# Zero products in TensorE's gaps, a K/V contraction in 256 columns, and a new order: grouped attention and a gated MLP with their gradients, on one core

## The chip, the cores and the metric

One NeuronCore of one Trainium2 chip. The time is device microseconds of one execution, median of several; lower is better. The core has TensorE (PE, with weight loads listed apart as PEld), VectorE (DVE), ScalarE (ACT), GpSimd (POOL) and SyncE (SP), which here issues nearly all DMAs from one queue. TensorE writes to PSUM; ScalarE and VectorE copy from there to SBUF ("eviction"), and DMAs move data between SBUF and the chip's main memory.

## What is computed

The forward pass of a decode block and its gradients for a given `grad_out`:

```
xn = layernorm(x)                                  # x: 2 x 1 x 576
q  = xn @ wq                                       # 32 query heads of 128, 16 K/V heads
o  = softmax(q k^T / sqrt(128)) v                  # K, V: 2 x 16 x 4096 x 128
out = x + o @ wo + ((xn @ w_gate) * (xn @ w_up)) @ w_down
outputs: out, d x, d k_cache, d v_cache, d wq, d wo, d w_gate, d w_up, d w_down
```

With one query token per batch entry there is little arithmetic for each byte. K and V (32 MB each) are read once, their gradients (32 MB each) are written once, and so are the weights and their gradients: 92.48 MB are read and 92.48 MB written.

## The kernel before

**Work.** There are 16 steps `s`, each for one batch entry and a group of two K/V heads. A step loads two K tiles and two V tiles of 1 MB (`load_kv`), turns them with VectorE's 32x32 transposes (`turn`, line 1156), forms scores with K and dP with V on TensorE (`score`, line 1205, 32 products of 128 columns for one head), does the softmax and its gradient in small instructions of all engines (`softmax`, `dscore`), and then two kinds of larger work:

- `contract(s, t)` (lines 1361 to 1400): P times V for the output (t = 1) and dS times K for dq (t = 0). Sixteen products of 512 columns run in two parts of eight (line 1378), four side by side in column groups of 32. They write the PSUM tile `ct`; an eviction of 512 columns takes it to `osb`, and four small products with the constant `fold` (line 1395) sum it up. After the products the K or V tiles are free for the next load (`free_kv`).
- `outer` and `head_outer` (line 1226): the gradients of K and V, outer products of 512 columns into a PSUM tile of two banks, evicted in 1024 columns (lines 422 and 424) to a 1 MB tile that SP stores (`put`, line 644).

The projections and the MLP (`group_front`, `group_back`, `mlp`) have the same form: weights are loaded, products are formed, the weights' gradients are outer products (lines 675, 712, 756 and others) and are stored. PSUM has three tiles `o` of two banks and two tiles `m` of one bank; all 1 MB tiles of loads and stores come from one ring of 16 (`big`).

**Order.** Nothing is ordered by hand. Every piece of work is a generator that yields what it needs: an engine with a cost in microseconds (`PE`, `ACT`, `DVE`, `POOL`, `EV` for an eviction on the engine that is done earlier), a DMA, a ring's slot (`ACQ`, `REL`), an event (`WAIT`, `SET`). `Order.run` (line 153) replays them in a model of time when the kernel is built: of the streams that can go on it takes the earliest, and among those of one engine within a slack the one with the best priority (`PRI`, lines 256 to 293; `AT` says after which K/V load a weight's load goes). The instructions are emitted in that order, and on the chip each engine and SP's queue keep it. Real waits are by semaphores, which follow from the tiles that an instruction reads and writes; the replay's times only set the order. A product's cost in the replay is

```
def PE(stream, issue=0.0, quad=None, kind="f"):
    return ("op", "PE", max(CLK * stream, issue) + 0.03, quad, stream, issue, kind)
```

where `stream` is the time at TensorE's full clock and `CLK` is 1.65 (line 301). `EV(512)` is billed at 0.585 us on ScalarE (line 222).

Of the kernel before, what the change touches and what calls it, by code (L numbers as in the profile page):

```python
# [13 lines left out]
P = 128  # L14
# [13 lines left out]
class Stream:  # L28
    def __init__(self, gen, prio, ready):
        self.gen, self.prio, self.ready = gen, prio, ready  # L30
        self.req = None
        self.land = None

# [30 lines left out]
class Order:  # L64
# [3 lines left out]
    def __init__(self):  # L68
# [8 lines left out]
        self.lanes = []  # L77

# [74 lines left out]
    def run(self):  # L153
        while self.streams:
# [12 lines left out]
            if r[0] in ("op", "any"):  # L167
                cost = r[2] if r[0] == "op" else next(c for x, c, _ in r[1] if x == e)
                quad = r[3] if len(r) > 3 else None
                if e == "PE":  # L170
                    end = t + cost + self.TAIL
# [7 lines left out]
                s.ready = end + self.HOP  # L179
# [4 lines left out]
            elif r[0] == "acq":  # L184
# [3 lines left out]
                i = min((k for k, v in slots.items() if v is not None), key=lambda k: (when(slots[k]), k))  # L188
                slots[i] = None
# [59 lines left out]
def DMA(engine, cost, nbytes, row=8192):  # L249
# [7 lines left out]
    "turn0": [12127.5, 6592.3, 21769.7, -2605.1, 16027.7, 11327.0, 15999.3, 39550.4, 10382.6, -7734.4, 35538.2,  # L257
        24878.1, 2718.9, 31584.2, -26890.5, 2784.8],
    "turn1": [-17638.3, 2610.3, 11642.0, -23025.1, -666.2, 15183.7, -8429.9, 1153.7, -20487.3, 25941.4,
        10117.7, 4947.3, -2272.2, 26485.5, 30929.5, -2450.0],  # L260
    "W0": [17499.7, 23187.9, 23229.4, -24562.1, -25413.4, 21241.8, -52583.1, 25355.3, -4026.7, -26992.9,
        -2792.0, -39509.0, -20712.1, -23397.7, -38581.5, -1973.1],
    "W1": [-68220.0, -3785.6, -5692.6, -26672.7, -32830.2, -16110.0, -12761.0, -19860.2, 22087.6, 15126.8,
        -21980.3, 8805.5, -32643.6, 50340.4, -9766.7, -46949.6],
    "BD0": [33847.1, 15885.5, -3782.4, -11229.3, 24201.3, 31507.4, 16705.2, 36715.7, 22613.4, -26234.1,
        -2581.7, 109848.8, -44765.9, -8040.0, -3442.2, 23039.7],
    "BD1": [6023.1, 63457.9, 25871.9, 3200.3, 32198.5, -18814.1, 12365.4, 26532.9, 45847.1, -51895.6, 27362.3,
        -76393.3, 2863.2, -15443.1, -42340.1, -14044.7],
    "att": [-30329.0, -12134.6, -9680.1, 2262.2, -4349.2, 5413.2, -20317.8, -14023.7, -15815.4, -22206.1,
        -49797.4, -334.9, -19593.2, -20211.8, -68161.8, -27358.0],  # L270
    "dsc": [-23906.4, -34630.7, -2728.5, -23998.0, -19328.5, -8575.3, -10061.5, -15550.8, 13655.4, -23902.2,
        -28324.1, -40880.7, -28538.6, -56867.0, -5830.5, -12006.5],
    "conv": [-12341.8, -11809.0, -28772.8, 4652.6, -75297.7, -7012.1, -20664.5, 17461.5, 27449.8, 21658.4,
        -6850.8, -13921.3, -10206.6, -13431.8, 19855.6, -8570.5],
    "con": [-42900.2, 17788.3, 198.2, -17106.1, -21976.4, -3999.9, 7207.3, -22623.4, -6927.6, 21516.2, 20924.0,
        -13390.2, -118243.2, -7700.5, 19019.7, 14780.5],
    "out0": [22678.2, 12788.2, 42398.2, 31027.3, 49279.4, -11087.6, 5917.5, 42793.0, -20399.7, 57105.8,
        29375.6, 687.4, 24906.2, -2550.4, -27276.1, 33869.5],
    "out1": [19262.8, 2604.4, 2928.7, 23228.2, 21627.8, -10501.4, 15188.8, 7961.4, 18967.4, 20607.5, 11898.0,
        33332.1, 33685.2, 22220.0, 30731.2, 4846.1],  # L280
    "load": [27975.6, -31596.9, -27237.7, 3512.0, -22563.4, -17007.1, 4137.9, 25122.5, 5758.3, -9052.6,
        -35105.2, 2003.7, -28928.7, 6812.9, 23298.4, -60102.7],
# [6 lines left out]
    "wout": [-3917.3],  # L289
    "store": [6257.1],  # L290
    "fin": [-45349.8],
    "const": [46567.9],
}
AT = {
    "wq": [-5, 7, 11, 24, 31, -18, 50, -5],
# [5 lines left out]
CLK = 1.65  # L301
# [1232 lines left out]
```

## Time and profile before

| | |
|---|---|
| median of 3 runs | 472.44 us (471.49 to 472.63) |
| the profiled execution | 471.37 us |
| its span, first to last instruction | 469.6 us |
| mean granted TensorE clock | 0.71 |
| bytes moved by DMA | 185.96 MB, mean 396 GB/s |
| products on TensorE | 6636, each with a weight load |

Busy times are of the span. "PEclk" is the clock that TensorE was granted; in this trace it is 0.5 or 1.0 at any moment. "DMA" is the mean busy share of the core's 16 DMA engines; packets that overlap can bring it a little over 1. A "wait" is idle time of an engine put down to what ended it; "SPq" is SP's queue, whose waits are those of the DMAs to be issued. Matmuls are pipelined, so a product's time holds its way through the array, and bursts are better compared whole.

### The profile page before, as it was taken

What the parts mean: (1) busy time and instruction counts of PE and PEld (TensorE: products, weight loads), DVE (VectorE), ACT (ScalarE), POOL (GpSimd) and SP (SyncE); (2) the same over time, 40 slices, a digit from 0 to 9 for tenths busy, and PEclk for the clock granted to TensorE, in tenths of its full rate; (3) what the DMA queues carried; (4) which work ended last, traced back from release to release, by engine and by line L of the source; (5) the groups of instructions that cost most, each with busy time, mean ns of one, the idle gap of its engine ahead of it and who ended that gap; (6) DMA issues with size and microseconds to landing.
All of it is one profiled execution on the core that took longest, in us unless ns stands there. A gap on an engine that the chain in (4) does not pass through costs nothing.

```text
span 469.6 us, 15459 instructions
## 1 busy us (share of the span) xinstructions
PE 370.8 (79%) x6636; PEld 217.5 (46%) x6636; DVE 369.5 (79%) x705; ACT 334.3 (71%) x507; POOL 146.8 (31%) x176
## 2 busy tenths in 40 slices
PE   0588688869887777986997669789699898998984
PEld 0455444435653352554463444564345434444453
DVE  9689878967867879688689658978867978898772
ACT  2149668867885948671798638877678678789973
POOL 3350242681330320203252264000843705325100
PEclk9978897767757668776675767956656658566977
DMA  8999999999999999999999999999999989999995
GB/s 317 404 413 403 363 390 419 409 416 421 418 416 420 399 421 406 412 415 419 399 418 404 386 418 424 408 413 342 413 416 393 424 270 416 423 413 413 424 368 176
DMA packets 40053, 185.96 MB, mean 396 GB/s; under 512 B 3496, under 2 KB 11184, under 8 KB 23600
## 3 DMA queue, kind: packets, MB, share of 16 engines
q1 hardware_dynamic: 39976, 184.96, 98.1%
q8 instruction: 52, 0.85, 0.7%
q14 instruction: 17, 0.14, 0.1%
q10 hardware_dynamic: 8, 0.00, 0.0%
HBM read 92.48 MB, written 92.48 MB: 394 GB/s over the span
## 4 chain that ended last, share of the span: by engine, by line
PE 42%; ACT 18%; DVE 18%; DMA 12%; issue 5%; POOL 2%; SPq 2%; ACTq 0%; DVEq 0%; POOLq 0%
ACT big L422 15%; DMA out_dram<-big 10%; DVE big L418 8%; PE ps_m L1378 8%; PE ps_o L1226 7%; PE ps_m L1205 7%; PE ps_o L675 4%; PE ps_m L841 3%; DVE big L424 3%; DMA big<-in_A_v_cache_dram 3%; PE ps_m L967 2%; PE ps_m L636 2%; POOL BD L1193 2%; PE ps_o L712 1%; SPq L1129 1%
## 5 line engine op out<-in xcount | busy, mean ns | idle before, releaser
L422 ACT CAST big<-ps_o 128x1024 bf16<-128x1024 f32 (+4 forms) x319 | 279.7, 950 | 40.3 <-PE ps_o L1226 18.2
L418 DVE STREAM_TRANSPOSE big<-big 128x1024 f32<-128x1024 f32 x146 | 176.1, 1223 | 5.9 <-DMA big<-in_A_v_cache_dram 3.6
L1193 POOL TENSOR_TENSOR BD<-vr,mask 128x2048 bf16<-128x2048 bf16 x32 | 115.2, 3603 | 198.8 <-ACT vr L422 122.2
L424 DVE CAST big<-ps_o 128x1024 bf16<-128x1024 f32 (+2 forms) x71 | 78.2, 1102 | 15.8 <-PE ps_o L675 5.2
L1205 PE MATMUL ps_m<-big,W 128*32 128x128 bf16 x2048 | 57.1, 274 | 5.5 <-ACT osb L422 0.7
L1226 PE MATMUL ps_o<-BD,dd 32*128 32x512 bf16 x256 | 48.8, 489 | 12.7 <-ACT big L422 9.2
L1205 PEld LDWEIGHTS <-W 128*32 128x32 bf16 x2048 | 45.4, 121 | 21.9 <-issue 18.6
L1226 PE MATMUL ps_o<-BD,pp 32*128 32x512 bf16 x256 | 42.1, 461 | 10.4 <-ACT big L422 6.7
L1170 POOL COPY W<-rep 32x16 bf16<-32x16 bf16 x128 | 24.5, 192 | 63.5 <-DVE rep L951 53.2
L418 DVE STREAM_TRANSPOSE big<-ww 128x1152 f32<-128x1152 f32 (+1 forms) x25 | 32.9, 1317 | 4.5 <-DMA out_dram<-big 3.3
L1378 PE MATMUL ps_m<-big,pp 128*32 128x512 bf16 x256 | 28.2, 536 | 1.5 <-DVE small L1330 1.2
L1378 PE MATMUL ps_m<-big,dd 128*32 128x512 bf16 x256 | 27.5, 518 | 1.5 <-DVE dd L418 0.6
L1226 PEld LDWEIGHTS <-dd 32*128 32x128 bf16 x256 | 11.8, 97 | 32.4 <-issue 24.7
L1226 PEld LDWEIGHTS <-pp 32*128 32x128 bf16 x256 | 10.4, 95 | 26.9 <-issue 22.6
L422 ACT CAST osb<-ps_m 128x512 bf16<-128x512 f32 x15 | 8.9, 590 | 15.9 <-PE ps_m L1378 12.6
L675 PE MATMUL ps_o<-dyr,R 32*32 32x288 bf16 x256 | 17.3, 402 | 2.0 <-ACT big L422 2.0
L675 PE MATMUL ps_o<-dyr,hb 32*32 32x288 bf16 x288 | 16.5, 346 | 1.1 <-ACT big L422 0.9
L967 PE MATMUL ps_m<-big,Wdy 128*128 128x128 bf16 x144 | 14.9, 285 | 3.1 <-DVE small L1283 2.0
L712 PEld LDWEIGHTS <-xnr 32*128 32x128 bf16 x368 | 12.5, 119 | 9.3 <-issue 8.6
L422 ACT CAST sp<-ps_m 128x256 bf16<-128x256 f32 x22 | 8.4, 380 | 11.2 <-PE ps_m L1213 11.0
L636 PEld LDWEIGHTS <-wm 128*32 128x32 bf16 x704 | 13.4, 115 | 6.3 <-issue 5.1
L841 PE MATMUL ps_m<-big,Wdy 128*128 128x128 bf16 x162 | 15.6, 272 | 0.6 <-DVE small L1291 0.4
(210 smaller groups left out, 481.9 us busy)
## 6 DMA issues: line engine op xcount, KB each, us to landing
out_dram<-big SPq DMA_DIRECT2D x74, 1024.0 KB, 12.1
big<-in_A_k_cache_dram SPq DMA_DIRECT2D x32, 1024.0 KB, 12.4
big<-in_A_v_cache_dram SPq DMA_DIRECT2D x32, 1024.0 KB, 12.5
out_dram<-big SPq DMA_DIRECT2D x17, 576.0 KB, 11.4
ww<-in_B_w_down_dram SPq DMA_DIRECT2D x9, 576.0 KB, 11.1
ww<-in_A_wo_dram SPq DMA_DIRECT2D x8, 576.0 KB, 11.1
ww<-in_A_wq_dram SPq DMA_DIRECT2D x8, 512.0 KB, 11.6
big<-in_B_w_gate_dram SPq DMA_DIRECT2D x4, 1024.0 KB, 13.1
```

What stands on the lines that cost most here:

```text
L418: nc.vector.transpose(out, in_)
L422: nc.scalar.copy(out, in_)
L424: nc.vector.tensor_copy(out=out, in_=in_)
L636: nc.tensor.matmul(dp[32 * q:32 * q + 32, :], lhsT=view(Wm[:], 0, P, 8 * pos(q, s), [[1, 32]]), rhs=view(X, 0, P, xoff(q, s), [[FS, blocks ...
L675: nc.tensor.matmul(o[32 * q:32 * q + 32, aa, 0:HD2], lhsT=view(t, 32 * q, 32, 2 * A + aa, [[4, 32]]), rhs=dyr[32 * q:32 * q + 32, k * HD2: ...
L841: nc.tensor.matmul(dh, lhsT=Wdy[:, e, 2 * k:2 * k + P], rhs=view(X[:], 0, P, 64 * k + e, [[D, FC], [2, 32]]), start=(k == 0 and e == 0), s ...
L967: nc.tensor.matmul(dp, lhsT=Wdy[:, e, 2 * k:2 * k + P], rhs=view(X[:], 0, P, 64 * k + e, [[D, GH], [2, 32]]), start=(k == 0 and e == 0), s ...
L1170: nc.gpsimd.tensor_copy(view(W_t[t][w][:], 32 * a, 32, 6 + 8 * a, [[G * WW, 4], [WW, G], [1, 2]]), view(rep_t[grp[g]["qs"]][:], 32 * a, 32 ...
L1193: nc.gpsimd.tensor_tensor(BD_t[i][:], view(vr_t[v][:], 0, P, 0, [[0, 16], [1, Dh]]), view(mask16[:], 0, P, 0, [[1, 16], [0, Dh]]), ALU.mult)
L1205: nc.tensor.matmul(sc[32 * cq:32 * cq + 32, :], lhsT=view(W[:], 0, P, (be * G + l) * WW + 6 - 4 * c2 - 2 * l, [[1, 32]]), rhs=view(X[:], 0 ...
L1226: nc.tensor.matmul(o[:, k, :], lhsT=pr2[32 * c4:32 * c4 + 32, :], rhs=BD[32 * c4:32 * c4 + 32, 8 * l + 4 * h2:8 * l + 4 * h2 + 4, :], star ...
L1378: nc.tensor.matmul(ct[32 * j:32 * j + 32, :], lhsT=view(rT, 0, P, 4 * c + 2 * l, [[1, 32]]), rhs=kv_t[kvS[s][t][l]][:, Dh * c:Dh * (c + 4) ...
```

## The change

Three things are changed together.

*Zero products.* Ahead of each group of products, `Order.run` looks for an idle gap of TensorE in the replay and for a PSUM tile (`m` or `o`) that is free in it, or the tile that the stream has just taken. It emits `keep`: products of a stationary of zeros (`none`, 128x128) with four copies of the identity, 512 columns, into that tile. Their number is 0.8 of the gap, less 0.05 us, over 0.1079 x CLK us, at most 40. The replay's times do not change by it.

*The contraction.* It runs in 256 columns in place of 512: 32 products in place of 16, `osb` half as wide, an eviction of 256 columns, and two products with `fold`. In the replay it also waits for the landing of its K or V tiles (`kvL`).

*The order.* All priorities, three of the slacks and biases, and the places of the weights' loads have new values. A column of PSUM that the softmax uses moves from 256 to 128.

```diff
@@ class Order
+        self.idle, self.spare, self.fill = 0, None, lambda tag, i, n: None
...
                 if e == "PE":
+                    self.idle = 0
+                    spare = [(self.slots[g][i], g, i) for g in ("m", "o") for i in self.slots[g] if self.slots[g][i] is not None]
+                    spare = min(spare + s.own, key=lambda x: x[0], default=None)
+                    if spare:
+                        gap = t - max(self.free[e], spare[0]) - FILL[0]
+                        self.idle = min(40, int(FILL[1] * gap / (FILL[2] * CLK))) if gap > 0 else 0
+                        self.fill(spare[1], spare[2], self.idle)
+                        self.spare = spare[1:] if spare not in s.own else None
                     end = t + cost + self.TAIL
...
-                s.ready = end + self.HOP
+                s.ready, s.own = end + self.HOP, []
...
+                s.own = [(slots[i], r[1], i)] if r[1] in ("m", "o") else []
                 slots[i] = None
...
 PRI = {
-    "turn0": [12127.5, 6592.3, 21769.7, ...
+    "turn0": [9201.5, 2578.1, 27143.9, ...
...
 AT = {
-    "wq": [-5, 7, 11, 24, 31, -18, 50, -5],
-    "wo": [-13, -2, -15, 2, 36, -14, 47, 53],
-    "mlp": [2, 16, -13, 39, 111],
+    "wq": [-8, 6, 9, -14, 30, 18, 42, 29],
+    "wo": [0, 3, -18, -19, -3, 14, 49, -5],
+    "mlp": [2, 17, 29, 40, 125],
 }
...
-BIAS = 0.21111771427708687
-SLACK = {"PE": 0.0, "ACT": 0.11786185086953341, "DVE": 0.44815392421950667, "POOL": 1e9, "SP": 1e9}
+FILL = (0.05, 0.8, 0.1079)
+BIAS = 0.19830938226133488
+SLACK = {"PE": 0.0, "ACT": 0.005924738677576517, "DVE": 0.6124175840724267, "POOL": 1e9, "SP": 1e9}
...
-    osb_t = tiles("osb", 1, [P, 4, P])
+    osb_t = tiles("osb", 1, [P, 2, P])
...
+    none = filled("none", [P, P], BF16, 0.0)
+
+    def keep(tag, i, n):
+        for _ in range(n):
+            nc.tensor.matmul(m_t[i][:] if tag == "m" else o_t[i][:, 0], lhsT=none[:],
+                             rhs=view(ident[:], 0, P, 0, [[0, 4], [1, P]]), start=True, stop=True)
+
+    od.fill = keep
...
@@ contract
-        yield WAIT(Ezero, grp[g]["EoT"])
+        yield WAIT(Ezero, grp[g]["EoT"], *kvL[s][t])
...
-        ct = m_t[m]
+        ct = m_t[m][:, 0:256]
...
-            yield PE(0.427, 0.056, kind="c")
-            for k in range(8 * part, 8 * part + 8, 4):
+            yield PE(0.427, 0.42, kind="c")
+            for k in range(8 * part, 8 * part + 8, 2):
                 for j in range(4):
                     c, l = k + NCH // 2 * (j // 2), j % 2
                     nc.tensor.matmul(ct[32 * j:32 * j + 32, :], lhsT=view(rT, 0, P, 4 * c + 2 * l, [[1, 32]]),
-                                     rhs=kv_t[kvS[s][t][l]][:, Dh * c:Dh * (c + 4)],
-                                     start=(k == 0), stop=(k == NCH // 2 - 4))
+                                     rhs=kv_t[kvS[s][t][l]][:, Dh * c:Dh * (c + 2)],
+                                     start=(k == 0), stop=(k == NCH // 2 - 2))
...
-        e = yield EV(512)
+        e = yield EV(256)
...
-        for w in range(4):
-            nc.tensor.matmul(m_t[m][:, 0:GH], lhsT=osb_t[i][:, w], rhs=fold[:, w], start=(w == 0), stop=(w == 3))
+        for w in range(2):
+            nc.tensor.matmul(m_t[m][:, 0:GH], lhsT=osb_t[i][:, w], rhs=fold[:, w], start=(w == 0), stop=(w == 1))
```

More of the change, by code (lines that the diff above doesn't have):

```diff
@@ L32, in __init__ @@
         self.land = None
+        self.own = []
 class Landing:
@@ L478 @@
     mask16 = const.tile([P, 16], BF16, name="mask16")
-    fold = const.tile([P, 4, GH], BF16, name="fold")
-    foldf = ch_t[0]["ex"][:, 80:80 + 4 * GH].rearrange("p (w r) -> p w r", w=4)
+    fold = const.tile([P, 2, GH], BF16, name="fold")
+    foldf = ch_t[0]["ex"][:, 80:80 + 2 * GH].rearrange("p (w r) -> p w r", w=2)
     Exn, Exr, Edy, Econst, Ezero = Event(), Event(), Event(), Event(), Event()
```

80 lines of the change are left out of this document (40 added, 40 removed).

## The prediction, made before the changed kernel ran

> **What bounds the kernel now.** I read the page's head first: engines, clock and DMA.
>
> ```profile
> span 469.6 us, 15459 instructions
> PE 370.8 (79%) x6636; PEld 217.5 (46%) x6636; DVE 369.5 (79%) x705; ACT 334.3 (71%) x507; POOL 146.8 (31%) x176
> PEclk9978897767757668776675767956656658566977
> q1 hardware_dynamic: 39976, 184.96, 98.1%
> ```
>
> No engine is busy above 79%, but the queue that carries all loads and stores is busy for 98.1% of the span. The kernel is bound by its DMAs; a change of TensorE can win only where the DMA runs dry. TensorE's granted clock is low, so I looked at it beside the DMA in stretches that I chose where the page's GB/s dips (columns: busy time of PE, weight loads, DVE, ACT and POOL, then PEclk, DMA share, GB/s).
>
> ```profile
> 40.00:64.00 24.00, 19.07 (x441) 12.83 (x441) 21.55 (x40) 17.00 (x27) 5.14 (x9) 0.79 0.99 373
> 64.00:250.00 186.00, 150.74 (x2831) 90.98 (x2827) 147.30 (x261) 137.25 (x211) 58.82 (x73) 0.70 1.02 414
> 250.00:264.00 14.00, 10.50 (x178) 5.50 (x177) 13.57 (x20) 10.43 (x16) 5.14 (x9) 0.68 0.96 383
> 310.00:330.00 20.00, 17.34 (x329) 9.43 (x325) 15.12 (x27) 14.57 (x22) 0.27 (x1) 0.59 0.97 366
> 376.00:380.00 4.00, 4.00 (x56) 1.59 (x55) 3.90 (x6) 2.50 (x4) 0.00 (x0) 0.50 0.48 150
> 380.00:390.00 10.00, 8.66 (x98) 4.54 (x97) 7.05 (x15) 8.59 (x14) 1.53 (x8) 0.67 0.98 351
> 456.00:460.00 4.00, 3.71 (x132) 2.60 (x127) 1.98 (x8) 3.10 (x6) 0.00 (x0) 0.90 0.44 164
> ```
>
> Against 414 GB/s, the rate of the long stretch, the others fall short by (414 - rate) / 414 of their length: 40 to 64 us by 2.4 us, 250 to 264 by 1.0, 310 to 330 by 2.3, 376 to 380 by 2.6, 380 to 390 by 1.5. That is 9.8 us inside the run; 456 to 460 loses 2.4 us in the tail. These are all there is to win: about 12 us, 2.6% of the span.
>
> Who made the largest hole? SP's own waits between 355 and 380 us, its issues, and TensorE at that time:
>
> ```profile
> SPq L1087 <- PE ps_m L1378: 8.5, 2, 7.8
> ...
> 378.41 0.34 SPq L1087 DMA_DIRECT2D big<-in_A_v_cache_dram  x1
> ...
> 376.00 1.05 PE L1378 MATMUL ps_m<-big,pp 128*32 128x512 bf16 x8 [0.25 <-DVE small L1330]
> 377.30 1.04 PE L1378 MATMUL ps_m<-big,pp 128*32 128x512 bf16 x8
> ```
>
> The next V load stood 7.8 us on the queue for a buffer that the K/V contraction (line 1378) frees; the contraction ended at about 378.3 and the load went out at 378.41. TensorE was busy for all 4.00 us of that stretch, at clock 0.50. So here it is a slow TensorE that starves the DMA. The chain agrees that TensorE is the longest part of what the DMA waits for:
>
> ```profile
> PE 42%; ACT 18%; DVE 18%; DMA 12%; issue 5%; POOL 2%; SPq 2%; ACTq 0%; DVEq 0%; POOLq 0%
> ```
>
> **The change, part by part.** *1. The zero products.* They are there for the clock alone, so first: what is the clock worth, and what sets it? The same eight products of line 1378 at full and at half clock, the longest wait of a product after the start, and a fall of the clock in windows of 3.41 us:
>
> ```profile
> 291.81 0.61 PE L1378 MATMUL ps_m<-big,dd 128*32 128x512 bf16 x8
> 318.11 1.05 PE L1378 MATMUL ps_m<-big,pp 128*32 128x512 bf16 x8
> PE ps_m L1328 <- DVE small L1322: 5.8, 4, 2.5
> 296.38:299.80 3.42, 3.27 (x54) 2.35 (x52) 3.42 (x7) 3.42 (x8) 0.00 (x0) 1.00 1.01 419
> 299.80:303.21 3.41, 1.10 (x16) 0.49 (x13) 3.29 (x5) 3.41 (x5) 0.00 (x0) 1.00 1.00 413
> 303.21:306.62 3.41, 2.89 (x92) 2.67 (x92) 2.95 (x7) 1.05 (x3) 0.00 (x0) 0.50 1.03 418
> 310.04:313.45 3.41, 3.24 (x78) 2.57 (x68) 2.73 (x7) 3.41 (x6) 0.00 (x0) 0.50 1.00 410
> 316.86:320.28 3.42, 3.25 (x38) 0.98 (x38) 1.57 (x4) 1.58 (x4) 0.00 (x0) 0.50 0.93 372
> 320.28:323.69 3.41, 2.57 (x92) 2.09 (x88) 3.32 (x8) 3.25 (x5) 0.00 (x0) 1.00 0.97 347
> ```
>
> Eight products of 512 columns, four side by side, are two passes. They take 1.05 us at half clock and 0.61 at full: 0.44 us for two passes, so one pass of 512 columns costs about 0.22 us at full clock and 0.44 at half. A window with only 1.10 us of work is followed by half clock; at half clock windows with up to 3.24 us busy keep it, and one with few, long products ends it. So the gate seems to weigh how much streams through the array, not only whether it is busy. A fill is the heaviest product there is, 128 rows by 128 columns by 512, so it counts by either measure, unless zeros don't count. Many of today's stationaries and BD blocks are mostly zeros as well, and the clock does rise beside them. I take it that the fills raise the mean clock from 0.71 to 0.85 or more.
>
> [...]
>
> How many fills? The replay fills 0.8 of a planned gap and bills 0.1079 x 1.65 = 0.178 us for each. Measured idle is 469.6 - 370.8 = 98.8 us, so 98.8 x 0.8 / 0.178 gives some 450, an estimate; the replay's own gaps stand in no trace, and I keep 250 to 700. They cost 450 x 0.22 = 99 us at full clock, 198 at half. Does that fit? At clock 0.71 some 58% of the time is half clock. If 58% of the 370.8 busy us shrink as line 1378 does (0.61 / 1.05), busy time falls by 90 to 281, idle grows to 189, and 99 us fit twice. At half clock they do not fit, but then TensorE is full of heavy products, and the window rows say that this brings the clock back. Behind a fill the whole of TensorE is queued, so a fill that starts late delays the next real product; this is covered by what lies ahead in the DMA queue:
>
> ```profile
> out_dram<-big SPq DMA_DIRECT2D x74, 1024.0 KB, 12.1
> q8 instruction: 52, 0.85, 0.7%
> ```
>
> A store lands 12.1 us after its issue, and 1 MB takes 1.05 / 0.414 = 2.5 us, so four or five transfers are in flight: TensorE can be late by several us before the DMA notices. A fill also waits for its tile's last reader, a wait that stood elsewhere before; the tile is the one that the replay has free longest, so I count nothing for it (bounds 0 and +1 us).
>
> What the clock then wins: the dips where TensorE was slow and its clock low, 376 to 390 and 310 to 330 (2.6 + 1.5 + 2.3 = 6.4 us), of which I take three quarters, **-4.8 us**. The dips of 40 to 64 and 250 to 264 I leave: VectorE was busy 90% and 97% there. In the tail:
>
> ```profile
> 452.83 1.87 PE L1440 MATMUL ps_o<-identf,acc 128*2 128x64 f32 x16
> 454.92 1.15 PE L675 MATMUL ps_o<-dyr,R 32*32 32x288 bf16 x16
> 456.33 0.98 PE L675 MATMUL ps_o<-dyr,R 32*32 32x288 bf16 x16 [0.26 <-ACT big L422]
> 458.23 6.12 SPq L644 DMA_DIRECT2D out_dram<-big  x6
> ```
>
> These three bursts lead to the store that went out only at 458.23. At full clock they lose 0.42 of 4.0 us: **-1.7 us**.
>
> *2. At the start* TensorE is idle up to its first product at 5.5 us and again to 11.7, and the clock is presumably still low:
>
> ```profile
> 5.51 0.63 PE L534 MATMUL ps_o<-xy,ex 2*128 2x288 bf16 x2 [5.51 <-DVE identf L489]
> 11.66 0.29 PE L580 MATMUL ps_m<-ident,BD 2*128 2x2 bf16 x4 [5.51 <-DVE BD L571]
> ```
>
> Some 20 fills for a gap of 5 us would end about 3 us late at half clock. The next product waits for VectorE till 11.66 anyway, which covers it. If it did not, +3 us of start would be lost; I take 0.
>
> *3. The contraction in 256 columns.* Sixteen products become 32 with the same columns streamed, so no time on TensorE. The eviction and its share of ScalarE and VectorE halve:
>
> ```profile
> L422 ACT CAST osb<-ps_m 128x512 bf16<-128x512 f32 x15 | 8.9, 590 | 15.9 <-PE ps_m L1378 12.6 <-DVE small L1322 3.3
> L422 ACT CAST sp<-ps_m 128x256 bf16<-128x256 f32 x22 | 8.4, 380 | 11.2 <-PE ps_m L1213 11.0
> ```
>
> 32 evictions x (590 - 380) ns = 6.7 us of eviction time. Nothing that the DMA waits for hangs on this tile (the buffer is freed by the products, ahead of the eviction), so I count 0, at best -1 us. Four fold products become two (0 on the path). More instructions: 32 x 16 products for the contraction, less 64 for the fold, plus 450 fills are some 900 products with their weight loads, 1800 on top of 15459. That is 12% of 0.85 MB, 0.1 MB or **+0.25 us** of DMA.
>
> *4. The wait for K/V* changes the replay's order only: the product waits for that load on the chip anyway, and TensorE's waits of before hold none for a DMA at line 1378. 0.
>
> *5. The new order* moves every instruction, SP's queue too. Its dips will lie elsewhere; the trace cannot say how large they are. Bounds from today's: none left of the 3.4 us that I did not count, or two more holes like 376 to 380 (+5.2). I take 0, since the same DMA work is spread by the same rules.
>
> Sum: -4.8 - 1.7 + 0.25 = -6.2 us. The profiled execution took 471.37 us (its span of 469.6 and 1.8 around it); it comes to 465.1. The median of the runs shown, 472.44, is 1.07 above it: **466.2 us**, -1.3%.
>
> **Rivals.** *The DMA hides it* (472, within 0.3%): the clock rises, or it does not, but the holes move to where VectorE and ScalarE are the late ones. For it: DMA share 1.02 over the 186 us stretch, at clock 0.70. Against it: the 7.8 us wait for line 1378.
>
> *The fills make TensorE late* (477 us, slower). One mechanism: the number of fills is fixed at 0.178 us each, but one takes 0.44 at half clock. In 10 us of half clock with 3 planned as idle, 13 fills take 5.7 us instead of 3, and 7 us of real products planned at 1.65 take 2.0 / 1.65 as long, 1.5 more: TensorE loses 4 us per 10. From some 25 to 30 us of unbroken half clock, or less where the DMA queue is short, the 12 us in flight are used up. Price: two holes like 376 to 380 beside those of today, +5.2 us. For it: today's half clock lasts for 17 us on end (303 to 320). Against it: the fills themselves should end such stretches.
>
> *Zeros do not count at the gate* (about 520 us): the clock stays 0.71 and 450 fills cost 0.58 x 0.44 + 0.42 x 0.22 = 0.35 us each, 157 us for 98.8 us of idle; TensorE becomes the bound, +58 us less what its waits absorb.
>
> **How the numbers follow.** Forecast (461 to 471) 0.55; hidden 0.14; late TensorE or a worse order (474 to 482) 0.25; zeros do not count 0.06. About 0.3% is what a measurement of this kernel can tell from no change, so faster is under 471.0 and slower over 473.9: 0.55, 0.14, 0.31. The forecast's own range: all 12 us of holes less instructions to only a third of the sum, 461 to 471. The range for 8 in 10 reaches into the slower rival up to 478 and leaves out its upper end (0.08), the zeros (0.06) and what lies below 461 (0.04).
>
> **What would show it.** Right: PEclk at 9 in nearly all slices, line 1378's bursts (now 16 products) at about 0.6 us, no stretch under 200 GB/s before the tail, DMA share over 98.1%. Wrong: PEclk as before with PE above 95% busy (zeros); PEclk high but the same 10 us of holes with SP waiting for ACT or DVE (hidden); SP waiting for a PE line behind a group of fills (late TensorE). What would break it most simply is a new order with a hole of its own.

## The result, and the profile after

The changed kernel is slower by 0.6%: 475.50 us median (473.58 to 476.38, 7 runs) against 472.44 for the kernel before in the same session, a ratio of 1.0061 (95% interval 1.0036 to 1.0086). 466.2 us was forecast. The profiled execution took 476.38 us, its span 474.5.

The page of the changed kernel: head, clock, rates, queues, chain. (Its line numbers are 20 higher than before: the contraction is L1398, the fills are L456, a store is L664, a K/V load L1107.)

```profile
span 474.5 us, 17012 instructions
PE 414.5 (87%) x7406; PEld 235.0 (50%) x7406; DVE 374.2 (79%) x717; ACT 322.5 (68%) x494; POOL 147.4 (31%) x176
PEclk9995698977879879979888995986797779698769
GB/s 295 402 412 396 318 419 363 416 409 420 422 424 411 418 385 378 418 418 422 412 371 419 358 392 401 424 411 397 421 418 422 420 416 425 424 389 236 423 362 199
q1 hardware_dynamic: 39976, 184.96, 97.4%
q8 instruction: 58, 0.95, 0.7%
DMA 40%; PE 31%; ACT 13%; DVE 9%; issue 4%; POOL 1%; SPq 0%; ACTq 0%; POOLq 0%; DVEq 0%
```

The bytes are the same, the queue of loads and stores is busy 97.4% of a longer span, so the DMA had more idle time and not more work. The mean granted clock rose from 0.71 to 0.84, but 5 and 6 still stand in PEclk. The chain, the work that ended last followed back from the end, now has its largest share in DMAs (40%, it was 12%). The rates show where the DMA ran dry: 318 in slice 5, 363 and 358 in slices 7 and 23, 236 in slice 37.

The groups of the fills, and the contraction's eviction on ScalarE (busy and mean ns behind the count, then the idle time ahead of them):

```profile
L456 PE MATMUL ps_o<-ident,none 128*128 128x512 bf16 x193 | 56.5, 407 | 0.8 <-ACT big L434 0.5
...
L456 PE MATMUL ps_m<-ident,none 128*128 128x512 bf16 x129 | 42.8, 459 | 2.2 <-POOL ident masks.py:199 1.4 <-DVE small L1311 0.4 <-DVE rep L971 0.4
...
L434 ACT CAST osb<-ps_m 128x256 bf16<-128x256 f32 x14 | 5.3, 380 | 13.0 <-PE ps_m L1398 12.9
```

There are 322 fills, 99.3 us of busy time. TensorE's busy time rose by only 43.7 us, because the real products ran at a higher clock: without the fills it is 315.2 us, 370.8 before.

What SP's queue waited for, before and then after (us in total, times, longest):

```profile
SPq L1087 <- PE ps_m L1378: 16.5, 7, 7.8
SPq L1087 <- DMA out_dram<-big: 16.0, 10, 3.4
```

```profile
SPq L1107 <- DMA out_dram<-big: 48.6, 22, 5.6
...
SPq L1107 <- PE ps_m L1398: 9.1, 5, 3.0
```

The wait of the prediction's argument, a load behind the contraction, did shrink (16.5 to 9.1 us). The loads now wait longer for earlier stores to land (48.6 us, it was 16.0), so part of TensorE's gain ends at the DMA.

Slice 5 (47 to 59 us) shows most, together with what leads up to it. TensorE between 31 and 47 us:

```profile
31.48 0.62 PE L1398 MATMUL ps_m<-big,pp 128*32 128x256 bf16 x16
...
35.81 0.41 PE L902 MATMUL ps_m<-hT,ww 128*128 128x2 bf16 x11
38.02 0.40 PE L902 MATMUL ps_m<-hT,ww 128*128 128x2 bf16 x9 [1.80 <-issue]
...
45.01 1.04 PE L1398 MATMUL ps_m<-big,dd 128*32 128x256 bf16 x16
```

Sixteen products of 256 columns take 0.62 us at full and 1.04 at half clock, as eight of 512 did (0.61 and 1.05). At 36.22 us TensorE stopped in the middle of a group of 20 equal products, for 1.80 us, and nothing that the profile shows released it ("issue"). Such a wait is called a stand below. From then on the clock is 0.50, and some 4 us later the DMA starves (columns: busy time of PE, weight loads, DVE, ACT, POOL, then PEclk, DMA share, GB/s):

```profile
34.00:38.00 4.00, 2.15 (x83) 1.58 (x82) 2.05 (x6) 2.08 (x3) 0.02 (x1) 0.98 1.04 407
38.00:42.00 4.00, 3.51 (x27) 1.71 (x27) 3.45 (x7) 3.00 (x4) 0.00 (x0) 0.50 1.01 416
42.00:46.00 4.00, 4.00 (x48) 2.71 (x50) 3.63 (x8) 3.48 (x4) 0.00 (x0) 0.50 0.86 355
46.00:50.00 4.00, 3.83 (x128) 2.64 (x117) 2.61 (x5) 2.91 (x6) 0.00 (x0) 0.74 0.80 264
50.00:54.00 4.00, 4.00 (x84) 2.21 (x80) 4.00 (x7) 3.92 (x7) 0.00 (x0) 0.69 0.90 330
```

Against 414 GB/s the stretch from 42 to 54 us loses 0.57 + 1.45 + 0.81 = 2.8 us. The kernel before loses 1.7 us in the same stretch:

```profile
42.00:54.00 12.00, 9.41 (x249) 5.38 (x246) 10.43 (x21) 10.20 (x16) 0.00 (x0) 0.93 0.98 355
```

So this place makes up only some 1.1 of the 5.0 us by which the two profiled executions differ. SP's queue of the changed kernel shows the load that came late:

```profile
34.18 10.77 SPq L664 DMA_DIRECT2D out_dram<-big  x3
48.04 0.34 SPq L1107 DMA_DIRECT2D big<-in_A_k_cache_dram  x1
```

### The profile page after: what moved, and what is told of

Its sections match the earlier page's. It is cut to its first block, busy times and chain, and to the rows that moved or that the text cites. A ratio compares the mean times of both kernels' runs of the same rounds, so it can differ in the third digit from the quotient of the medians.

```text
span 474.5 us, 17012 instructions
## 1 busy us (share of the span) xinstructions
PE 414.5 (87%) x7406; PEld 235.0 (50%) x7406; DVE 374.2 (79%) x717; ACT 322.5 (68%) x494; POOL 147.4 (31%) x176
## 3 DMA queue, kind: packets, MB, share of 16 engines
q1 hardware_dynamic: 39976, 184.96, 97.4%
## 4 chain that ended last, share of the span: by engine, by line
DMA 40%; PE 31%; ACT 13%; DVE 9%; issue 4%; POOL 1%; SPq 0%; ACTq 0%; POOLq 0%; DVEq 0%
DMA out_dram<-big 22%; DMA big<-in_A_v_cache_dram 12%; ACT big L434 12%; PE ps_m L456 6%; DMA big<-in_A_k_cache_dram 6%; DVE big L430 6%; PE ps_o L1246 4%; PE ps_m L1398 4%; PE ps_m L1225 3%; PE ps_o L695 2%; PE ps_o L456 2%; DVE big L436 2%; PE ps_m L656 2%; PE ps_m L861 1%; PE ps_o L776 1%
## 5 line engine op out<-in xcount | busy, mean ns | idle before, releaser
L434 ACT CAST big<-ps_o 128x1024 bf16<-128x1024 f32 (+2 forms) x316 | 277.1, 953 | 50.1 <-PE ps_o L1246 28.3
L436 DVE CAST big<-ps_o 128x1024 bf16<-128x1024 f32 (+3 forms) x74 | 81.2, 1099 | 13.6 <-PE ps_o L695 5.5
L456 PE MATMUL ps_o<-ident,none 128*128 128x512 bf16 x193 | 56.5, 407 | 0.8 <-ACT big L434 0.5
L1225 PE MATMUL ps_m<-big,W 128*32 128x128 bf16 x2048 | 47.4, 241 | 2.5 <-DVE oT L1418 2.1
L456 PEld LDWEIGHTS <-none 128*128 128x128 bf16 x322 | 30.6, 107 | 35.1 <-issue 17.7
L1225 PEld LDWEIGHTS <-W 128*32 128x32 bf16 x2048 | 36.6, 104 | 18.2 <-issue 16.5
L456 PE MATMUL ps_m<-ident,none 128*128 128x512 bf16 x129 | 42.8, 459 | 2.2 <-POOL ident masks.py:199 1.4
L1398 PE MATMUL ps_m<-big,dd 128*32 128x256 bf16 x512 | 25.0, 331 | 0.9 <-DVE small L1287 0.7
L1246 PEld LDWEIGHTS <-dd 32*128 32x128 bf16 x256 | 11.5, 93 | 28.3 <-issue 23.9
L1398 PE MATMUL ps_m<-big,pp 128*32 128x256 bf16 x512 | 23.3, 305 | 0.4 <-DMA big<-in_A_v_cache_dram 0.3
L1398 PEld LDWEIGHTS <-dd 128*32 128x32 bf16 x512 | 13.0, 110 | 8.1 <-issue 4.1
L1398 PEld LDWEIGHTS <-pp 128*32 128x32 bf16 x512 | 12.7, 104 | 7.2 <-issue 4.0
```

Of the source, the lines that this page charges most:

```text
L434: nc.scalar.copy(out, in_)
L436: nc.vector.tensor_copy(out=out, in_=in_)
L456: nc.tensor.matmul(m_t[i][:] if tag == "m" else o_t[i][:, 0], lhsT=none[:], rhs=view(ident[:], 0, P, 0, [[0, 4], [1, P]]), start=True, sto ...
L1225: nc.tensor.matmul(sc[32 * cq:32 * cq + 32, :], lhsT=view(W[:], 0, P, (be * G + l) * WW + 6 - 4 * c2 - 2 * l, [[1, 32]]), rhs=view(X[:], 0 ...
L1246: nc.tensor.matmul(o[:, k, :], lhsT=pr2[32 * c4:32 * c4 + 32, :], rhs=BD[32 * c4:32 * c4 + 32, 8 * l + 4 * h2:8 * l + 4 * h2 + 4, :], star ...
L1398: nc.tensor.matmul(ct[32 * j:32 * j + 32, :], lhsT=view(rT, 0, P, 4 * c + 2 * l, [[1, 32]]), rhs=kv_t[kvS[s][t][l]][:, Dh * c:Dh * (c + 2) ...
```

## The experiments

Three things change together, so each was run alone and in all combinations. The order was held fixed by giving the replay the same costs whatever is emitted: in each kernel that is said to have the old or the new order, each engine and SP's queue issue the same work in the same sequence as the kernel that it is compared with (fills and split products aside). Ratios are to the kernel before, run beside each, with 95% intervals.

The theories at the outset: the gain is lost in the **order** (holes of its own); the **fills** make TensorE late; the **256 columns** cost something by their width; or they cost by their **code**, that is by twice the number of TensorE instructions.

### The parts one by one

The fills alone (old order, 512 columns; the zeros are one column that the product reads 128 times):

```diff
+    none = filled("none", [P, 1], BF16, 0.0)
...
+            nc.tensor.matmul(..., lhsT=view(none[:], 0, P, 0, [[0, P]]), rhs=view(ident[:], 0, P, 0, [[0, 4], [1, P]]), ...)
...
+    od.fill = keep
```

> The kernel before with the zero products and nothing else: the same order on all engines, contraction in 512 columns. If the new order is what costs (theory O), this gains as was forecast: about 467 us, ratio 0.985 to 0.993, and a clock of 0.85 or more. If the fills make TensorE late (theory F): about 475 us, 1.005 or more. If the DMA hides TensorE whatever its clock (theory H): 471 to 474, 0.997 to 1.003.

The columns alone (old order, no fills; the replay still bills 512):

```diff
-            for k in range(8 * part, 8 * part + 8, 4):
+            for k in range(8 * part, 8 * part + 8, 2):
...
-                                     rhs=kv_t[kvS[s][t][l]][:, Dh * c:Dh * (c + 4)],
+                                     rhs=kv_t[kvS[s][t][l]][:, Dh * c:Dh * (c + 2)],
```

> The kernel before with the contraction in 256 columns alone; the replay is given the old costs, so that the order is that of before. O, F and H all expect no change: ratio 0.997 to 1.003. If the 512 more products cost by themselves (theory C): 1.005 or more, with bursts of line 1398 longer than the 1.05 us at half clock that eight products of 512 columns took.

The changed kernel with the old order (priorities, slacks, loads' places and replay costs of before):

> All of the change but the order: fills and 256 columns in the order of before. O: 466 to 468 us, 0.985 to 0.993, some 8 us under the changed kernel. F: about 475, as the changed kernel. H: 471 to 474, as before.

The changed kernel without fills:

```diff
-    od.fill = keep
```

> The changed kernel without its zero products: the new order, 256 columns, the clock back at about 0.71. O: slower still than the changed kernel, about 480 us, 1.012 to 1.02 of before, as the fills' gain is lost. F: faster than the changed kernel, about 470. H: about 475, as the changed kernel, since only the order counts.

The changed kernel with 512 columns (its order and its fills kept; to make room, the zeros are again one column that is read 128 times):

> The changed kernel, its order and its fills, with the contraction back in 512 columns (the replay is given the new costs, so the order is that of after). If the columns are the cost and the order is neutral: 0.995 to 0.999, as the fills alone in the old order (0.9968). If the new order costs beside the columns (theory O): 1.001 to 1.004.

The same without fills, by the same edit as above:

> The changed kernel's order with 512 columns and without fills, the last cell of order, fills and columns. With fills it was 0.9957, without fills in 256 columns 1.0046. If the order is neutral and the fills bring 0.3 to 0.4%: 0.998 to 1.002. If the new order itself is what is better: 0.994 to 0.997, and the fills bring nothing there.

The cells together:

| order, columns | no fills | fills |
|---|---|---|
| old, 512 | 1 (before) | 0.9968 (0.9948 to 0.9988), 470.99 us |
| old, 256 | 1.0044 (1.0027 to 1.0061), 473.81 us | 1.0037 (1.0017 to 1.0058), 473.88 us |
| new, 512 | 1.0031 (1.0004 to 1.0057), 472.95 us | 0.9957 (0.9938 to 0.9977), 468.94 us |
| new, 256 | 1.0046 (1.0024 to 1.0069), 473.61 us | 1.0061 (1.0036 to 1.0086), the change |

A difference of two cells is uncertain by some 0.3 points. Compared cell by cell, the narrow contraction costs 0.44 points in the old order without fills, 0.69 with them, 0.15 in the new order without and 1.04 with them. The fills win 0.32 and 0.74 points with 512 columns, and with 256 nothing that can be measured (-0.07 and +0.15). The order has no steady sign: +0.31, -0.11, +0.02, +0.24. So the **columns** turn the forecast gain into a loss, though the 0.15 alone could be nothing, and the new order with fills and 512 columns beats both kernels. In the cells with fills the layout of the zeros changes along with the columns; in those without fills, and in the run with a narrow step 0 below, it does not.

None of the first theories came out whole. Order as the cause asked for 0.985 to 0.993 in the old order (measured 1.0037) and for 1.012 or more without fills (1.0046). Late fills asked for 1.005 or more from the fills alone (0.9968). The columns alone came out at 1.0044, under the 1.005 that a cost of their own asked for, and without the longer bursts that it asked for.

### Width or code?

512 columns as before, but 16 empty products of one column of zeros, added into a column that they leave as it is, go into each contraction: 512 more products, where 256 columns have 448 more, without their width.

```diff
+                    if k > 0:
+                        nc.tensor.matmul(ct[32 * j:32 * j + 32, 0:1], lhsT=view(none[:], 0, P, 0, [[0, 32]]), rhs=ident[:, 0:1],
+                                         start=False, stop=False)
...
+                    if k == 0:
...
```

> The kernel before, in its order, with 16 zero products of one column added to each contraction: as many instructions as the contraction in 256 columns has, but eviction, tile and columns as before. The columns alone cost 1.0044 (1.0027 to 1.0061), and every stall of TensorE without a releaser there ended 1.2 to 1.5 us after a 16 KB packet of the instruction queue. If more instructions cost because TensorE waits for its code (theory I): the same, 1.003 to 1.006, and 4 us or more of such stalls. If the 256 columns cost by themselves (theory W: the eviction's new time, the smaller tile): 0.998 to 1.002.

Measured 1.0053 (1.0030 to 1.0076), 474.56 us. The empty products are not quite free by themselves: a part's burst takes 0.68 us at full and 1.11 at half clock where it took 0.62 and 1.05, some 4 us over the 64 bursts. So this run alone does not part the count from TensorE's time. The opposite, 256 columns with every second product left out (half of the K/V sum is missing), so that the count is about that of before (64 fewer) and the streamed columns are half; the edit is shown against the kernel with the columns alone:

```diff
-            for k in range(8 * part, 8 * part + 8, 2):
+            for k in range(8 * part, 8 * part + 8, 4):
```

> The kernel of the columns alone, with every second group of products of the contraction left out (half of the sum over K and V is not formed): 256 columns, but no more instructions than before, and half of the columns streamed. I: the cost is gone, 0.996 to 1.001, stalls for code under 2.5 us. W: still 1.003 or more.

Measured 0.9958 (0.9935 to 0.9981), 469.58 us: with the count of before the loss is gone. Part of its gain may be the work left out. And the dose, 128 columns (four times the products of before, in the old order, without fills):

```diff
+            for k in range(8 * part, 8 * part + 8):
...
+                                     rhs=kv_t[kvS[s][t][l]][:, Dh * c:Dh * (c + 1)],
```

> The kernel before, in its order and without fills, with the contraction in 128 columns: 64 products in place of 16 for one contraction, the same columns streamed, an eviction of 128 columns. Code on TensorE grows by 2880 instructions where 256 columns added 896. If TensorE's code is the cost (theory I): about three times the 0.44% of 256 columns, 1.010 to 1.016, with 8 us or more of stalls that end behind a packet of the instruction queue. If only the form in 256 columns costs (theory W), the smaller eviction is no worse: 1.000 to 1.006.

Measured 1.0243 (1.0210 to 1.0275), 482.86 us. 512, 256 and 128 columns give 1, 1.0044 and 1.0243; the streamed columns are the same in all three. The products added are 448 and 1440, 3.2 times as many, and the cost is 5.5 times as high, above the 1.010 to 1.016 expected. The page, TensorE's waits and TensorE around one of them, all of the kernel with 128 columns:

```profile
q8 instruction: 63, 1.03, 0.8%
...
PE 46%; DVE 17%; ACT 16%; issue 9%; DMA 9%; SPq 2%; POOL 1%; DVEq 0%; ACTq 0%; POOLq 0%
```

```profile
PE ps_m L1224 <- issue: 13.8, 7, 2.7
PE ps_m L1397 <- issue: 6.0, 5, 2.0
```

```profile
69.45 0.63 PE L1397 MATMUL ps_m<-big,dd 128*32 128x128 bf16 x32
69.91 0.95 PE L1224 MATMUL ps_m<-big,W 128*32 128x128 bf16 x50
73.52 0.61 PE L1224 MATMUL ps_m<-big,W 128*32 128x128 bf16 x14 [2.66 <-issue]
```

Thirty-two products of 128 columns take 0.63 us at full clock, no more than eight of 512. But in the middle of a burst of equal products (L1224, the scores) TensorE stands for 2.66 us, and such stands add up to 21.1 us in 15 places (13.8 + 6.0 and 1.3 in two other lines); in the kernel before they are 1.9 us in 3. On the chain "issue" has 9%, 5% in the kernel before.

What does TensorE wait for there? The queue that carries instructions moved 1.03 MB in 63 packets, 16,384 bytes each; before, 0.85 MB in 52. TensorE's products and weight loads are 2 x 8076 = 16,152 here and 2 x 6636 = 13,272 before: 256 and 255 for each packet. In all 84 stands that the 20 traces hold, TensorE went on 1.2 to 1.6 us after the end of such a packet: 1.43, 1.46 and 1.38 us in the three of the kernel before, 1.42 us in the one at 36.22 us of the changed kernel. So a packet looks like TensorE's code for some 256 products and weight loads. What a packet that comes late costs stands in no trace by itself.

So these runs point to the count of instructions and not to the width: streaming and bursts stay the same, and the cost comes and goes with the count. That the stands are TensorE waiting for its code is **argued**, from the packets' number and from those that end ahead of every stand; no run took the fetching away alone. That the stands are the whole cost is **not shown**. One execution of each kernel gives, in us:

| from, to | stands, from and to | time added |
|---|---|---|
| old order, no fills: 512 to 256 | 1.9, 5.3 | 2.1 |
| the same: 512 to 512 with empty products | 1.9, 5.5 | 2.5 |
| the same: 512 to 128 | 1.9, 21.1 | 11.5 |
| new order, no fills: 512 to 256 | 0.6, 2.0 | 0.7 |
| old order, fills: 512 to 256 | 3.7, 5.5 | 3.3 |
| new order, fills: 512 to 256 (the change) | 1.0, 1.8 | 4.9 |

Without fills the added time is some 0.5 to 0.7 of the added stands. With fills it is more than they add up to: the changed kernel has a single stand, that of 1.80 us, less than the 1.9 us of the kernel before, and yet the columns cost it 4.9 us. There a stand can matter only by where it lies.

Two runs tried to move the stands by shifting the code. Sixty-four products of one column at the very start, in the kernel with the columns alone:

> The kernel of the columns alone with 64 products of one column (zeros) ahead of everything, while TensorE is idle: every later instruction sits half a 256-instruction block further on. I: the stalls for code fall at other instructions and the time moves by some 1 to 2 us, either way, from the 1.0044 of the columns alone. W: no change from it, 1.003 to 1.006.

Measured 1.0038 (1.0015 to 1.0062), 473.07 us, against 1.0044 unshifted; the stands lie elsewhere and sum to 5.2 us (5.3 unshifted). The 1 to 2 us that late code was expected to move did not show. And the changed kernel with its first 52 fills cut into two of 256 columns (104 instructions more):

> The changed kernel, with its first 52 fills each cut into two of 256 columns: the same columns at the same places, and every later instruction sits 104 instructions further on in the 256-instruction blocks of code. In the changed kernel's trace TensorE stands for 1.80 us at 36.2 us, in the middle of twenty products of line 902, until 1.42 us after a packet of the instruction queue, and its DMAs are late from there on. If that stall starts the loss (theory I): the stall moves away from 36 us and the time falls to 468 to 473 us, ratio 0.994 to 1.002, unless another falls before 60 us. If it is the 256 columns or the order (W, O): as the changed kernel, 1.003 to 1.009.

Measured 1.0094 (1.0070 to 1.0118), 475.71 us. The stand at 36.22 us was replaced by one at 34.61 and there are three more, 4.6 us in all. Neither run freed the kernel of stands, so neither tells whether it would be faster without.

### Where in the run the columns cost

The changed kernel with 512 columns in the two contractions of step 0 alone, 56 instructions fewer of 17,012 (the other 30 contractions keep 256; tiles and zeros as in the 512-column kernel), and the reverse, 256 columns in step 0 alone:

```diff
+def CW(s):
+    return 4 if s == 0 else 2
...
+        cw = CW(s)
+            for k in range(8 * part, 8 * part + 8, cw):
```

> The changed kernel with 512 columns in the contractions of the first step alone (two of 32; 56 instructions fewer), 256 in the other 30. If the loss is made by code in the first 60 us, where the DMA has nothing ahead: 0.996 to 1.001, near the 0.9957 of 512 columns everywhere. If code costs wherever it is dense: 1.003 to 1.009, as the changed kernel.

> The other way round: 256 columns in the two contractions of the first step, 512 in the other 30, order and fills of the changed kernel. If the loss is made in the first 60 us: 1.002 to 1.008. If it is spread over the run: 0.995 to 0.998, as 512 everywhere.

Measured 0.9994 (0.9971 to 1.0016), 471.31 us, and 1.0012 (0.9984 to 1.0041), 472.51 us. With all at 256 it is 1.0061, with all at 512 0.9957. So of the 1.04 points, 0.67 go when step 0 alone is wide, and 0.55 come when step 0 alone is narrow (each with some 0.3 of uncertainty); the second run lies between what the two theories expected. The windows agree. Of the kernel with 512 columns throughout, and then of the one with 256 in step 0 alone:

```profile
42.00:46.00 4.00, 3.37 (x114) 1.95 (x107) 2.95 (x5) 3.48 (x5) 0.00 (x0) 0.96 1.00 420
46.00:50.00 4.00, 3.85 (x102) 2.31 (x103) 3.93 (x7) 4.00 (x7) 0.00 (x0) 0.90 1.00 408
50.00:54.00 4.00, 4.00 (x48) 2.11 (x48) 3.29 (x8) 2.79 (x6) 1.45 (x1) 0.68 1.07 408
```

```profile
42.00:46.00 4.00, 4.00 (x56) 2.98 (x58) 3.63 (x8) 3.48 (x5) 0.00 (x0) 0.50 0.90 373
46.00:50.00 4.00, 3.83 (x130) 2.73 (x119) 2.75 (x6) 2.99 (x5) 0.00 (x0) 0.82 0.77 252
50.00:54.00 4.00, 3.77 (x110) 2.13 (x101) 4.00 (x8) 4.00 (x7) 0.00 (x0) 1.00 0.83 280
```

Against 414 GB/s the first loses 0.1 us there, the second 3.3, the changed kernel 2.8. In the second, as in the changed kernel, TensorE stood at this place (35.9 to 37.8 us) and the clock was 0.50 afterwards; in the first it stood too, for 0.69 us. In the first the same K load went out 4.3 us earlier than the changed kernel's 48.04 (1.0 us of that is older: the store ahead of it went out at 33.16 and 34.18):

```profile
43.77 0.34 SPq L1107 DMA_DIRECT2D big<-in_A_k_cache_dram  x1
```

The clock goes with the late load. The first stretch of half clock behind 35 us lasts 10.2 us in the changed kernel (37.9 to 48.1), and as long in all four kernels with fills and a narrow step 0. In eight of the nine executions with 512 columns throughout, empty products aside, it lasts 3.4 us, and 6.8 in the ninth, that with half the fills. Without fills, 256 columns show 6.8 us twice and, with the shifted code, no half clock before 51 us. With step 0 alone wide it also lasts 6.8 us, behind a stand of 0.79 us, and that kernel still loses 1.2 us from 42 to 54 us:

```profile
42.00:54.00 12.00, 11.05 (x254) 6.19 (x253) 10.90 (x22) 10.64 (x16) 0.00 (x0) 0.88 1.01 373
```

Half clock for 6.8 us more leaves some 3.4 us of TensorE's work undone, an estimate that comes to the lateness of the load. Whether the stand or the narrow products themselves keep the clock down is not separated by any run.

With that load late the DMA share falls to 0.80 and 0.77, so little else lay in the queue to cover it. That later stands cost less because more is queued ahead is argued, not shown. The rest of the loss, some 0.4 points, comes later in the run, where the changed kernel has no stand; its cause stays open.

### The fills: how many, at the start, in the tail

The kernel with the new order and 512 columns with `FILL = (0.05, 0.4, 0.1079)`, 133 fills:

> As the changed kernel with 512 columns (0.9957), but with 0.4 of a gap filled in place of 0.8: 133 fills in place of 322. If the fills win by the clock alone and their own code costs little: less clock (0.76 to 0.82) and 0.996 to 0.999. If the fills' code eats half of what the clock brings (theory I): 0.992 to 0.996, as good or better with fewer of them.

Measured 0.9980 (0.9956 to 1.0004), 471.06 us, clock 0.75: between no fills (1.0031, 0.71) and all (0.9957, 0.86). The same kernel with its first 64 fills cut to one column, so that they take hardly any time (the first 33 take 1.02 us in place of 8.97):

> The new order with 512 columns (0.9957), its first 64 fills, those of the first 20 us, cut to one column each: the code stays as it is and the first products come at about 5.5 and 11.7 us again, not at 10.3 and 14.8. If the late start costs (a loss that was priced at nothing): 0.988 to 0.993. If VectorE and the loads cover it, as was forecast: 0.994 to 0.998; and if the early full clock is worth something: up to 1.000.

Measured 0.9987 (0.9963 to 1.0011), 470.66 us: the late start that the fills make costs nothing that can be measured.

The last question was where the fills' gain went. Single traces suggested the tail: with fills the burst of line 1460 came 4 us earlier, but the rest took 2 to 3 us longer, with fills on the chain. So the fills behind that burst were left out, in the new and in the old order (512 columns), beside a repeat of the best kernel:

```diff
+        od.fill = lambda tag, i, n: None
         yield from rows_put(o, 0, out_0)
```

> The new order with fills and 512 columns, but no fill behind the products of line 1460, where the tail begins (that burst began at 447.40 us in the same kernel with all fills, 19.5 us ahead of the end, and 17.3 us ahead of it without any fill). Theory: the run before the tail wins what the fills were forecast to win, and fills in the tail stand on the chain (0.54, 0.32, 0.32, 0.54 and 0.75 us there); without them the tail is 1 to 2 us shorter and the ratio 0.992 to 0.994. Rival: those fills only take the place of waits, and without them the clock falls; the tail stays as long and the ratio is 0.996 or more.

> The old order with fills and 512 columns, without the fills behind line 1460. With all fills that burst began at 448.17 us, 4.7 us ahead of the kernel before, and the rest took 19.8 us and not 16.8. Theory: without the tail's fills (0.75, 0.32 and 0.87 us on the chain) the rest takes 17 to 18.5 us and the ratio is 0.991 to 0.995. Rival, fills that take the place of waits: 0.997 as with them. A stall of 1.45 us in that tail may stay, as the code ahead of it is the same.

> The new order with fills and 512 columns once more, beside the run without the tail's fills on the same chip. 0.996 as before by either theory.

Measured 0.9975 (0.9949 to 1.0002), 470.26 us; 0.9988 (0.9966 to 1.0010), 470.71 us; and 0.9965 (0.9947 to 0.9984), 470.21 us. Nothing is won against 0.9957 and 0.9968 with them, so the theory of the tail's fills falls; the rival, by which they only take the place of waits, fits. The traces also warn: the same burst, behind the same instructions, began at 447.40 and 449.38 us in two executions of the best kernel, and at 451.56 without the tail's fills. A single execution places an event to some 2 us.

## Why the prediction was wrong

**The step that failed is part 3**, "Sixteen products become 32 with the same columns streamed, so no time on TensorE" with 0.1 MB of code at "+0.25 us of DMA". The bytes were right (0.85 to 0.95 MB) and the bursts are equally long. But the price of instructions isn't their bytes. In place of 0.25 us, the columns alone cost 0.44% (2.1 us), and with the new order and fills 1.04% (4.9 us), about half of it or more in step 0; empty products cost the like (1.0053). The cost was listed as traffic of the DMA engines, where it is 0.1 of 186 MB, and never as time in which TensorE stands. How the 4.9 us come about is shown only in part: the late K load of step 0 is, the rest is open. The trace of before had a row of the kind, a stand of 0.69 us inside a burst of 32 equal products:

```profile
49.28 0.41 PE L1205 MATMUL ps_m<-big,W 128*32 128x128 bf16 x13 [0.69 <-issue]
```

Forecast and result lie 9.3 us apart. The columns make 4.7 of that (4.9 and not 0.25). Some 4.5 more are in the fills and the order, which together won 2.0 us (0.9957) and not 6.5.

**The fills (part 1): mechanism right, size wrong.** Zeros count for the clock here: 0.71 to 0.82 in the old order, to 0.84 in the changed kernel (0.85 or more was forecast), so the rival in which they don't is refuted. Each is 128 rows by 128 columns by 512, four times the largest form of the kernel before; that the clock weighs what streams, as the prediction took it, no run shows by itself. There were 322, not 450 (276 in the old order). That they took the forecast 99 us all the same is luck: each took 0.31 us on average, not 0.22. The gain was forecast at 4.8 us inside the run and 1.7 in the tail; the fills alone won 0.32%, 1.5 us, and 0.74%, 3.5 us, in the new order. The same stretches in the kernel before, and then with the fills alone, show one execution's account:

```profile
64.00:150.00 86.00, 69.71 (x1299) 41.37 (x1296) 66.88 (x119) 65.58 (x101) 33.94 (x34) 0.72 1.02 417
...
250.00:310.00 60.00, 45.82 (x805) 27.56 (x807) 47.57 (x80) 42.43 (x64) 17.88 (x21) 0.70 1.01 408
310.00:330.00 20.00, 17.34 (x329) 9.43 (x325) 15.12 (x27) 14.57 (x22) 0.27 (x1) 0.59 0.97 366
330.00:376.00 46.00, 38.87 (x611) 20.96 (x600) 36.16 (x67) 34.44 (x52) 28.37 (x24) 0.61 1.02 412
376.00:390.00 14.00, 12.66 (x152) 6.13 (x152) 10.95 (x20) 11.08 (x17) 1.53 (x8) 0.62 0.84 293
```

```profile
64.00:150.00 86.00, 73.09 (x1272) 40.41 (x1274) 65.22 (x115) 65.22 (x100) 33.99 (x34) 0.78 1.01 412
...
250.00:310.00 60.00, 51.40 (x873) 28.91 (x872) 47.92 (x81) 42.87 (x62) 17.81 (x21) 0.78 1.02 417
310.00:330.00 20.00, 18.04 (x277) 8.88 (x268) 15.16 (x25) 12.93 (x21) 2.00 (x1) 0.60 0.99 384
330.00:376.00 46.00, 42.66 (x659) 21.04 (x662) 36.35 (x68) 35.97 (x53) 26.69 (x24) 0.78 1.01 403
376.00:390.00 14.00, 12.22 (x198) 6.51 (x199) 11.37 (x21) 10.74 (x19) 2.03 (x10) 0.88 0.95 357
```

By (change of rate) / 414 x length, the stretch from 376 to 390 wins 2.2 us, with the clock from 0.62 to 0.88: the hole on which the prediction rested closed by half, from 4.1 to 1.9 us. From 310 to 330 only 0.9 is won, and the clock stays at 0.60: TensorE is busy for 18.04 of 20 us there, and no fill stands ahead of 327 us. So the dips that the sum counted gave 3.1 us and not 4.8. 250 to 310 wins 1.3. But 64 to 150 and 330 to 376 lose 1.0 us each: part of the gain is given back in new, shallower dips, the "hidden" rival in part. And in the tail, where -1.7 us was to come from a full clock, TensorE stood 1.45 us on the chain and its last burst ran at half clock (1.86 us, 1.05 before):

```profile
456.36 0.62 PE L681 MATMUL ps_o<-Q,xnr 32*128 32x128 bf16 x11 [1.45 <-issue]
...
458.62 1.86 PE L1502 MATMUL ps_o<-identf,gg 128*2 128x64 f32 x16
```

The 1.7 was also a little large, as the third of its bursts, at 456.33 us, already ran at a mean clock of 0.75.

**The start (part 2): the 0 right, its reason not.** The fills run over further than forecast: there are 52 of them, not some 20, and the first products are 5.9 and 4.3 us late, so the wait for VectorE did not cover them. That the clock is still low there was a guess; the fills fit it, starting 0.43 us apart up to some 7 us and 0.22 us apart from then on. It is without cost all the same (shown with 512 columns, by the run with short fills at the start):

```profile
1.37 10.11 PE L456 MATMUL ps_m<-ident,none 128*128 128x512 bf16 x33 [1.37 <-POOL ident masks.py:199]
11.41 0.41 PE L554 MATMUL ps_o<-xy,ex 2*128 2x288 bf16 x2
11.76 4.27 PE L456 MATMUL ps_m<-ident,none 128*128 128x512 bf16 x19
15.97 0.29 PE L600 MATMUL ps_m<-ident,BD 2*128 2x2 bf16 x4
```

**The wait and the evictions (parts 3 and 4): right** that nothing comes of them, as far as the cells show: an eviction of 256 columns takes 380 ns on ScalarE as forecast, and no gain shows in any cell with 256 columns.

**The order (part 5): 0 was forecast**, and the four cells give +1.5 us to -0.5. It has a hole of its own, as the prediction's last sentence feared: 203 GB/s from 426 to 434 us of the changed kernel, in place of that from 376 to 380 before.

```profile
426.00:434.00 8.00, 5.24 (x63) 1.71 (x52) 6.98 (x10) 4.77 (x6) 0.00 (x0) 0.79 0.60 203
```

Every trace with the new order has this hole, with 512 columns too, so it doesn't make the change slower than the best version.

**The rivals.** The slower rival's 477 us lies nearer to the result than the forecast, but that is luck, as its mechanism isn't the cause: fills that make TensorE late would show between the cells with and without fills, and there the fills win (512 columns) or do nothing (256).

## What to carry to other kernels

Count TensorE's instructions as well as its columns: splitting the products was free in streaming time here (sixteen of 256 columns took 0.62 us, eight of 512 took 0.61) and still cost 0.4 to 1.0% in three of four cells, and in the changed kernel about half of that or more in the first of 16 steps. Look for idle time of TensorE that ends by nothing ("issue") inside a burst of equal products, and compare it with the packets of the instruction queue. A change of several parts is best run cell by cell with the order held fixed: here two of the three parts were worth keeping together (new order, fills, 512 columns: 0.9957, and 0.9965 when repeated), and the third took more than they gave.

## What the runs showed of the hardware

- During the run the instruction queue moves packets of 16,384 bytes, one for 255 (52 before) or 256 (63 with 128 columns) of TensorE's products and weight loads. TensorE stands for 0.15 to 2.7 us at a time, in all 84 cases of the 20 traces going on 1.2 to 1.6 us after the end of such a packet. That the packets are its code, and that it waits for it, is inferred from this.
- The clock did not follow busy time alone: it stayed at 0.50 from 38 to 46 us of the changed kernel while TensorE was busy for 3.51 and 4.00 of 4 us. Filling gaps with zero products of 128x128 by 512 columns raised its mean from 0.71 to 0.82 in the old order, to 0.84 in the changed kernel and to 0.86 in the new order with 512 columns; 133 of them in place of 322 raised it to 0.75.
- With 512 columns, fills that raised TensorE's mean clock from 0.71 to 0.82 and 0.86 won 0.32 and 0.74% in this kernel, whose DMA queue is busy 98.1% of the span before; beside the narrow contraction they won nothing measurable (-0.07 and +0.15 points).
